# Where 15 late additions of a bias row stand in VectorE's order, in a linear attention kernel with a feed-forward layer behind it

## The chip, the cores and the metric

The kernel runs on one core of a Trainium2 chip. Its time is device microseconds (us) of one execution; lower is better. All times inside the execution are counted from the start of its span, the time from the first to the last instruction that the profiler recorded.

## The reference

Gated linear attention for 4 batches of 8 heads, 768 steps, head size 48, and then a feed-forward layer with a squared relu, on 3072 tokens of 384 values:

```python
for t in range(S):
    state = alpha[:, :, t, :, None] * state + np.einsum('bhd,bhe->bhde', k[:, :, t], v[:, :, t])
    y[:, :, t] = np.einsum('bhd,bhde->bhe', q[:, :, t], state)
x = y.transpose(0, 2, 1, 3).reshape(B * S, H * D)
h = x @ w_in                     # 384 -> 2048
r = np.maximum(h, 0.0)
g = s * (r * r) + b              # s and b are single numbers
out = g @ w_out                  # 2048 -> 384
```

The number b adds the same row to every token's output: b times the column sums of w_out. The kernel computes this **bias row** once and adds it to the 384 output values of each token.

## The kernel before

The 3072 tokens are 24 blocks of 128 tokens, six to a batch. Each block n passes through these steps; the names are those of the functions in the code, and each is a handful of instructions:

- **load** (SP's DMA queue): alpha, k, q and v of a block, into rings of eight buffers.
- **ln**, **cum_pe**, **cum_act**: ScalarE takes logarithms of alpha, TensorE sums them along the block (L283), ScalarE makes the decays b and 1/b from them (L296, L297). cum_act also sends the last row of the decays through DRAM (**decay**, and **decay_in** back into `blast`), for the state.
- **kb_mul**, **qb_mul** (VectorE, L345 and L348; "kb" and "qb" below): k times 1/b and q times b.
- **tr** (TensorE, L356) transposes qb and kb into the PSUM bank `ct_ps`; **qk_copy** (VectorE, L368) copies both out at once. The next cum_pe writes into the same bank, so it comes after that copy.
- **amat** (TensorE, L389): the products of k and q, from that copy; **mask** (VectorE, L398), twice.
- **y_pe**, **pst_pe** (TensorE, L503 and L516): the block's output and its contribution to the state; **y_act** (ScalarE); **t1** (VectorE, L575/577) and **sd** (GpSimd, L587 and L591) carry the state on. The last block of a batch (n = 5, 11, 17, 23) has no t1 and sd.
- **vcast** (GpSimd, L278): v in bf16.
- **xt_pe**, **xt_act**: the output is transposed for the feed-forward layer.
- **mp**, **rl**, **sq** for each quarter u = 0 to 3 of the 2048 inner values: TensorE multiplies by w_in (L601, 12 matmuls), ScalarE takes the relu (L614), VectorE squares (L621; "square (n, u)" below).
- **o_pe** (TensorE, L632, four matmuls for a quarter): multiplies the squares by w_out, into the bank `o_ps`.
- **o_out**: for n of 15 and more, VectorE adds the bias row to the result as it takes it out of PSUM (L649), and it is stored. The first 15 blocks are done before the bias row is known: ScalarE puts their results as they are into `keep_sb`, which lies where the first copy of w_in was (`w_in_st`). Later **add_bias** (VectorE, L683) adds the row to each of the 15, in place, and **store** sends it to DRAM. A store of blocks 0 to 3 takes two DMAs, since their rows lie interleaved.

The bias row comes about as follows, all on VectorE: **colsum** (L206) adds up the parts of w_out, 128 x 768 at a time, eight blocks of time apart; **bias_sum** (L209) adds the two halves; **bias_turn** (L213 to L221) sums over the partitions by way of transposes; **bias_out** and **bias_in** send the row through DRAM so that it stands on all partitions, in four parts; **bias_add** 0 and 1 (L236, L238) add these parts into `bias_w`.

The order of the work is written out by hand. `at(pos, function, ...)` notes an event at a position, in which a block is 8 wide; all events are sorted by position (at the same position: in the order in which they were noted) and carried out once, so that each engine's queue, SP's DMA queue among them, gets its instructions in this order. Every engine works through its own queue in order. From block 10 on, even and odd blocks have position tables of their own (`places`), which make a repeating pattern of two blocks. With the events of `at` and these tables, VectorE's queue from position 133 to 138 reads as follows before the change:

```
133.00 add_bias 0   133.29 qk_copy 18   134.34 sq 16 0   134.34 sq 16 2   134.36 o_out 15
134.95 kb_mul 19    134.95 qb_mul 19    135.54 sq 16 1   135.79 sq 16 3   136.66 add_bias 1   137.71 qk_copy 19
```

TensorE's queue in the same stretch is: o_pe (15, 2), mp (16, 0), mp (16, 2), o_pe (15, 3), cum_pe 19, mp (16, 1), mp (16, 3), y_pe 17, o_pe (16, 0), tr 19, o_pe (16, 1), xt_pe 17, amat 18, amat 19, o_pe (16, 2). The pairs 20/21 and 22/23 follow the same pattern, 16 positions later each, with pst_pe behind y_pe there, and t1 of the block before ahead of the odd block's qk_copy.

Of the kernel before, what the change touches and what calls it, by code (L numbers as in the profile page):

```python
# [14 lines left out]
def kernel(  # L15
# [109 lines left out]
    NKEEP = 15  # L125
    keep_all = w_in_st.rearrange("a t f -> a (t f)")
    keep_sb = [keep_all[:, d_model * n : d_model * (n + 1)] for n in range(NKEEP)]
# [627 lines left out]
    def at(pos, fn, *args):  # L755
        events.append((pos, len(events), fn, args))
# [54 lines left out]

    for i in range(3, 8):
        at(69.3 + 8 * (i - 3), colsum, i)
    at(103.3, bias_sum)
    at(110.0, bias_turn)
    at(110.3, bias_out)
    at(111.4, bias_in)
    at(128.5, bias_add, 0)
    at(130.5, bias_add, 1)
    for n in range(NKEEP):  # L820
        at(133.0 + 3.66 * n, add_bias, n)
        at(133.9 + 3.66 * n, store, n, keep_sb[n])

    def late(pos, *what):
        for fn, *args in what:
# [75 lines left out]
```

## Time and profile before

| what | value |
|---|---|
| median of 3 runs | 185.82 us (185.32 to 186.15) |
| the profiled execution | 185.98 us |
| its span | 184.2 us |
| granted TensorE clock, mean | 0.998 |
| DMA, share of the span that the 16 engines were busy (q1) | 71.6% |
| add_bias (L683) | 15 times, 541 to 741 ns, from 128.9 to 174.2 us |
| o_out of the late blocks (L649) | 8 times, 543 to 551 ns |
| colsum, 128 x 768 (L206) | 6 times, 943 to 952 ns |
| bias_add 0, bias_add 1 | 1.26 us at 126.83, 0.75 us at 128.12 |

In the rows of the timeline, the columns are start and duration in us, engine, line, operation, what is written from what is read, shapes, the count of instructions drawn together, and in brackets idle time of the engine before it with what ended it. Engines are PE (TensorE), DVE (VectorE), ACT (ScalarE), POOL (GpSimd) and SP. Durations of neighbours on one engine overlap, since an instruction begins while the one before it is still finishing; the spacing of the starts says what an instruction costs its engine.

### The profile page before, as it was taken

What the parts mean: (1) busy time and instruction counts of PE and PEld (TensorE: products, weight loads), DVE (VectorE), ACT (ScalarE), POOL (GpSimd) and SP (SyncE); (2) the same over time, 40 slices, a digit from 0 to 9 for tenths busy, and PEclk for the clock granted to TensorE, in tenths of its full rate; (3) what the DMA queues carried; (4) which work ended last, traced back from release to release, by engine and by line L of the source; (5) the groups of instructions that cost most, each with busy time, mean ns of one, the idle gap of its engine ahead of it and who ended that gap; (6) DMA issues with size and microseconds to landing.
All of it is one profiled execution on the core that took longest, in us unless ns stands there. A gap on an engine that the chain in (4) does not pass through costs nothing.

```text
span 184.2 us, 6231 instructions
## 1 busy us (share of the span) xinstructions
PE 177.9 (97%) x2504; PEld 142.2 (77%) x2504; DVE 145.8 (79%) x308; ACT 122.1 (66%) x253; POOL 61.4 (33%) x97
## 2 busy tenths in 40 slices
PE   7888999999999999999999999999999999999993
PEld 2556899866698687787888878888778878878793
DVE  7599879666657588987898997778999899896541
ACT  3779797985678956656766765765755746734750
POOL 7338481110330625042505344144203343344000
PEclk9999999999999999999999999999999999999999
DMA  5999989989488989892985671989685945233322
GB/s 151 314 327 350 232 282 382 279 176 186 75 162 154 202 161 189 161 174 52 164 147 113 110 127 57 244 151 176 150 172 131 174 134 175 73 101 112 94 63 76
DMA packets 105934, 31.12 MB, mean 169 GB/s; under 512 B 98595, under 2 KB 104370, under 8 KB 105906
## 3 DMA queue, kind: packets, MB, share of 16 engines
q1 hardware_dynamic: 105902, 30.73, 71.6%
q8 instruction: 19, 0.31, 0.7%
q14 instruction: 9, 0.07, 0.1%
q10 hardware_dynamic: 4, 0.00, 0.0%
HBM read 25.98 MB, written 4.75 MB: 167 GB/s over the span
## 4 chain that ended last, share of the span: by engine, by line
PE 82%; DVE 9%; ACT 4%; issue 2%; POOL 1%; ACTq 0%; DVEq 0%; POOLq 0%
PE h_ps L601 26%; PE o_ps L632 25%; PE ct_ps L356 4%; PE h_ps L632 3%; PE o_ps L257 2%; PE a_ps L601 2%; PE ct_ps L601 2%; PE y_ps L503 2%; PE a_ps L389 2%; DVE gt_all L621 2%; PE ct_ps L283 2%; PE h_ps L555 2%; ACT bi_sb L296 2%; PE o_ps L601 2%; DVE qb_sb L348 1%
## 5 line engine op out<-in xcount | busy, mean ns | idle before, releaser
L601 PEld LDWEIGHTS <-w_in_bf 128*128 128x128 bf16 x1152 | 67.5, 98 | 4.9 <-issue 0.7
L614 ACT ACTIVATE r_sb<-h_ps 128x512 bf16<-128x512 f32 x79 | 47.0, 604 | 31.2 <-PE h_ps L601 29.5
L632 PE MATMUL o_ps<-w_out_bf,gt_all 128*128 128x384 bf16 x320 | 64.0, 326 | 0.0
L601 PE MATMUL h_ps<-xd_all,w_in_bf 128*128 128x128 bf16 x948 | 60.3, 219 | 0.0
L587 POOL TENSOR_TENSOR sd_sb<-t_sb,blast 48x192 bf16<-48x192 f32 x40 | 28.7, 718 | 83.5 <-DVE t_sb L577 56.1
L621 DVE TENSOR_TENSOR gt_all<-r_sb 128x512 bf16<-128x512 bf16 x96 | 40.9, 443 | 15.4 <-ACT r_sb L614 14.9
L632 PEld LDWEIGHTS <-gt_all 128*128 128x128 bf16 x368 | 32.5, 98 | 15.3
L278 POOL CAST v_bf<-v_sb 128x384 bf16<-128x384 f32 x23 | 15.1, 667 | 23.3 <-DMA v_sb<-in_v_dram 23.1
L345 DVE TENSOR_TENSOR kb_sb<-k_sb,bi_sb 128x384 bf16<-128x384 f32 x24 | 14.2, 594 | 7.7 <-ACT bi_sb L296 7.7
L562 ACT ACTIVATE xd_all<-h_ps 128x384 bf16<-128x384 bf16 x19 | 9.6, 503 | 9.6 <-PE h_ps L555 9.6
L348 DVE TENSOR_TENSOR qb_sb<-q_sb,b_sb 128x384 bf16<-128x384 f32 x24 | 13.7, 573 | 1.6 <-ACT b_sb L297 1.6
L267 ACT ACTIVATE la_sb<-al_sb 128x384 bf16<-128x384 f32 x24 | 12.5, 532 | 2.3 <-DVE blast L748 2.3
L591 POOL TENSOR_TENSOR sc_sb<-t_sb,blast 112x384 f32<-112x384 f32 x16 | 13.3, 830 | 1.3
L525 ACT ACTIVATE y_bf<-y_ps 128x384 bf16<-128x384 f32 x22 | 10.9, 497 | 3.2 <-PE y_ps L503 2.8
L368 DVE COPY qkT<-ct_ps 112x1024 bf16<-112x1024 bf16 x16 | 10.9, 684 | 1.9 <-PE ct_ps L356 1.8
L398 DVE TENSOR_TENSOR am_a<-a_ps,mask 128x512 bf16<-128x512 f32 x13 | 8.9, 686 | 3.2 <-PE a_ps L389 3.0
L296 ACT ACTIVATE bi_sb<-ct_ps 128x384 f32<-128x384 f32 x19 | 9.3, 489 | 2.5 <-PE ct_ps L283 2.4
L356 PEld LDWEIGHTS <-qb_sb 128*112 128x112 bf16 x96 | 8.2, 130 | 3.3 <-DVE qb_sb L348 1.8
L398 DVE TENSOR_TENSOR am_b<-a_ps,mask 128x512 bf16<-128x512 f32 x13 | 8.9, 682 | 1.7 <-PE a_ps L389 1.7
L297 ACT ACTIVATE b_sb<-ct_ps 128x384 f32<-128x384 f32 x19 | 9.4, 497 | 0.0
L683 DVE TENSOR_TENSOR w_in_st<-w_in_st,bias_w 128x384 f32<-128x384 f32 x15 | 8.3, 560 | 0.0
L356 PEld LDWEIGHTS <-kb_sb 128*112 128x112 bf16 x96 | 7.2, 130 | 0.7 <-DVE kb_sb L345 0.4
(146 smaller groups left out, 256.9 us busy)
## 6 DMA issues: line engine op xcount, KB each, us to landing
al_sb<-in_alpha_dram SPq DMA_DIRECT2D x20, 192.0 KB, 4.1
q_sb<-in_q_dram SPq DMA_DIRECT2D x20, 192.0 KB, 4.4
k_sb<-in_k_dram SPq DMA_DIRECT2D x20, 192.0 KB, 3.5
v_sb<-in_v_dram SPq DMA_DIRECT2D x20, 192.0 KB, 3.9
w_in_st<-in_moe_w_in_dram SPq DMA_DIRECT2D x4, 768.0 KB
w_out_st<-in_moe_w_out_dram SPq DMA_DIRECT2D x4, 768.0 KB
out_dram<-w_in_st SPq DMA_DIRECT2D x11, 192.0 KB, 1.9
out_dram<-out_sb SPq DMA_DIRECT2D x10, 96.0 KB, 1.6
```

The lines of the kernel that those rows point to most:

```text
L278: nc.gpsimd.tensor_copy(out=v_bf[n % 4], in_=raw("v", n))
L296: nc.scalar.activation(out=bi_sb[n % 2], in_=cv, func=AF.Exp, scale=-1.0)
L345: nc.vector.tensor_tensor(out=kb_sb[n % 4][:, :, 0:48], in0=raw("k", n), in1=bi_sb[n % 2], op=ALU.mult)
L348: nc.vector.tensor_tensor(out=qb_sb[n % 2][:, :, 0:48], in0=raw("q", n), in1=b_sb[n % 3], op=ALU.mult)
L356: nc.tensor.transpose(out=t_bank(n, x if n in pair_of else None)[0:112, x, p, :], in_=t.rearrange("a h d -> a (h d)")[:, 128 * p : 128 * p ...
L398: nc.vector.tensor_tensor(out=am_sb[e][n % 2], in0=a_bank(n)[e], in1=mask4, op=ALU.mult)
L587: nc.gpsimd.tensor_tensor(out=sd[r, :, d], in0=t1_sb[r, :, d], in1=bl[r].to_broadcast([48, NP, 48]), op=ALU.mult)
L591: nc.gpsimd.tensor_tensor(out=sc_sb[0:112], in0=t1_sb[0:112], in1=bl[0:112].to_broadcast([112, NP, 96]), op=ALU.mult)
L601: nc.tensor.matmul(out=hp[:, jj * C : (jj + 1) * C], lhsT=w_in_bf[:, kk, 128 * j : 128 * (j + 1)], rhs=xd_sb[n][:, kk], start=(kk == 0), s ...
L614: nc.scalar.activation(out=rs, in_=room((g, u)), func=AF.Relu)
L621: nc.vector.tensor_tensor(out=gt_sb[g][:, u * 512 : (u + 1) * 512], in0=rs, in1=rs, op=ALU.mult)
L632: nc.tensor.matmul(out=op[:, 0:d_model], lhsT=gt_sb[n][:, j * C : (j + 1) * C], rhs=w_out_bf[:, j, :], start=(j == 0), stop=(j == NJ - 1),)
```

## The change

In position terms: bias_sum goes from 103.3 to 101.4, right behind the last colsum (101.3); bias_add 0 from 128.5 to 127.55, right ahead of kb_mul 18; bias_add 1 from 130.5 to 133.4, behind qk_copy 18. The 15 additions, which stood 3.66 positions apart from 133.0 on, get positions from a list, and each store stands 1.5 behind its addition instead of 0.9.

```diff
-    at(103.3, bias_sum)
+    at(101.4, bias_sum)
     at(110.0, bias_turn)
     at(110.3, bias_out)
     at(111.4, bias_in)
-    at(128.5, bias_add, 0)
-    at(130.5, bias_add, 1)
-    for n in range(NKEEP):
-        at(133.0 + 3.66 * n, add_bias, n)
-        at(133.9 + 3.66 * n, store, n, keep_sb[n])
+    at(127.55, bias_add, 0)
+    at(133.4, bias_add, 1)
+
+    spare = [134.9, 134.95, 135.0, 143.55, 150.9, 150.95, 151.0, 159.55, 166.9, 166.95, 167.0, 172.5, 175.5, 178.5, 181.5]
+    assert len(spare) == NKEEP
+    for n, pos in enumerate(spare):
+        at(pos, add_bias, n)
+        at(pos + 1.5, store, n, keep_sb[n])
```

By the sorting, VectorE's queue from 133.29 to 137.71 is then:

```
133.29 qk_copy 18   133.40 bias_add 1   134.34 sq 16 0    134.34 sq 16 2   134.36 o_out 15   134.90 add_bias 0
134.95 add_bias 1   134.95 kb_mul 19    134.95 qb_mul 19  135.00 add_bias 2   135.54 sq 16 1   135.79 sq 16 3
137.71 qk_copy 19
```

Additions 4 to 6 stand in the same way in the next pair and 8 to 10 in the one after it; 3 and 7 stand between o_out and kb_mul of the even blocks 20 and 22; 11 ahead of square (21, 0), 12 between o_out 20 and square (21, 2), 13 and 14 ahead of square (22, 0).

## The prediction

> **What bounds the kernel now.** I read the busy row first, then the waits and the order in time of TensorE, then the same of VectorE where TensorE was late.
>
> ```profile
> PE 177.9 (97%) x2504; PEld 142.2 (77%) x2504; DVE 145.8 (79%) x308; ACT 122.1 (66%) x253; POOL 61.4 (33%) x97
> ```
>
> TensorE is busy 97% of the span, so a moved VectorE instruction can only count through a hole that it opens or closes in TensorE's row. From 95 us on I compared every matmul's start with the one before (o_pe 0.162 us, mp 0.055 us each). Apart from steps of 0.06 to 0.10 where the kind of matmul changes, four places are late. Three of them, in TensorE's rows (start, duration, idle before):
>
> ```profile
> 130.30 0.32 PE L283 MATMUL ct_ps<-la_sb,U_bf 128*128 128x384 bf16 x1 [0.30 <-DVE qkT L368]
> ...
> 147.88 0.40 PE L389 MATMUL a_ps<-qkT 48*128 48x128 bf16 x8
> 148.22 0.23 PE L389 MATMUL y_ps<-qkT 48*128 48x128 bf16 x1
> ...
> 161.86 0.40 PE L389 MATMUL a_ps<-qkT 48*128 48x128 bf16 x8
> 162.37 0.23 PE L389 MATMUL y_ps<-qkT 48*128 48x128 bf16 x1
> ```
>
> At 130.30 cum_pe 19 waits for qk_copy 18; its four predecessors began at 129.19 and need 4 x 0.162, so it is 0.46 late. In pairs without a hole, amat of the odd block starts 0.23 after amat of the even one (134.19 and 134.42). At 148.22 it is 0.34 (0.11 late), at 162.37 it is 0.51 (0.28 late), at 106.39 it is 0.45 (0.22 late). All four are VectorE's copies of transposed q and k (L368). So 1.07 us is all that a better order of VectorE can win from 95 us on.
>
> Now VectorE before one of them (blocks 18 and 21):
>
> ```profile
> 143.39 1.17 DVE L621 TENSOR_TENSOR gt_all<-r_sb 128x512 bf16<-128x512 bf16 x2 [1.00 <-ACT r_sb L614]
> 144.48 0.54 DVE L649 TENSOR_TENSOR out_sb<-o_ps,bias_w 128x384 f32<-128x384 f32 x1
> 144.95 0.54 DVE L345 TENSOR_TENSOR kb_sb<-k_sb,bi_sb 128x384 bf16<-128x384 f32 x1
> 145.41 0.55 DVE L348 TENSOR_TENSOR qb_sb<-q_sb,b_sb 128x384 bf16<-128x384 f32 x1
> 145.88 0.54 DVE L683 TENSOR_TENSOR w_in_st<-w_in_st,bias_w 128x384 f32<-128x384 f32 x1
> 146.35 0.74 DVE L621 TENSOR_TENSOR gt_all<-r_sb 128x512 bf16<-128x512 bf16 x2
> 147.02 0.54 DVE L577 TENSOR_TENSOR t_sb<-p_ps,sc_sb 112x384 f32<-112x384 f32 x1
> 147.49 0.67 DVE L368 COPY qkT<-ct_ps 112x1024 bf16<-112x1024 bf16 x1
> ```
>
> There is idle time only before the squares of the even block (1.00, ended by the relu). From the second square to the end of the copy, 148.16, VectorE runs without a gap, and TensorE goes on at 148.22. I call this the **odd chain**: two squares, o_out, kb, qb, two squares, t1, qk_copy. It starts when relu (18, 2) ends, which the new order doesn't change, and it has no room: TensorE already waits 0.11 for it.
>
> **The change, part by part.** Spacing is from one start to the next: 0.47 for an add (145.88 to 146.35), o_out, kb, qb or t1; 0.33 for a square; 0.65 from qk_copy to what follows. An instruction on TensorE follows its input's end by 0.05 (162.32 to 162.37).
>
> *bias_sum* leaves the place ahead of square (12, 1), where it made qk_copy 15 late, for the 0.45 of idle after colsum 7 (101.00 to 101.45). It has 0.47 to give back, the hole is 0.22: at best -0.22. But GpSimd is at work there:
>
> ```profile
> 101.45 1.74 DVE L621 TENSOR_TENSOR gt_all<-r_sb 128x512 bf16<-128x512 bf16 x2 [0.45 <-ACT r_sb L614]
> ```
>
> Two squares take 1.74 instead of 0.74, while GpSimd's state multiply (L591) runs from 101.44 for 0.83. Each shift of these squares up to 0.26 is free, one of 0.47 uses up all that bias_sum gave back, and 0.1 more makes tr 15 late. Bounds -0.22 and +0.1; I take -0.1, the middle. The Trainium skill (SBUF — State Buffer, Who interferes with whom) says that a VectorE instruction with two SBUF inputs and a GpSimd one that reads SBUF exclude each other, whoever is first, for the whole instruction. The stretched squares agree; by this rule bias_sum pushes GpSimd's multiplies, and so the squares behind them, back by its own length, and the term would be 0 instead of the -0.22 that the idle row alone would give.
>
> *bias_add 0* goes ahead of kb 18, where VectorE is idle 0.82 before 124.72. It waits for the bias row, whose four loads were issued by 114.0 and took 3.5, so it is there by 117.6, 6 us early. It costs 0.95 (the same shape in the colsum at 100.05), so kb 18 moves by some 0.1 and tr 18, 1 us later, sees nothing. *bias_add 1* goes behind qk_copy 18, into the idle time before the squares. qk_copy 18 then starts when tr 18 is done, about 127.4 instead of 129.57, and the 0.46 hole at 130.30 closes.
>
> *add_bias 0 to 2, 4 to 6, 8 to 10* come in threes into the odd chains of the pairs 18/19, 20/21 and 22/23: two between o_out and kb, one behind qb. Each of these chains held one add before. So 0.94 more stands in each; the idle 1.00 lies ahead of the relu, and the adds lie behind it, so it hides nothing.
>
> - Pair 18/19 (the chain holds no t1). Relu (16, 2) ends at 130.05, so square (16, 2) starts at 130.08, o_out 130.42, adds 130.89 and 131.36, kb 131.83, qb 132.30, add 132.77, squares 133.24 and 133.57, qk_copy 133.90 to 134.58. TensorE, freed of its 0.46, would be at tr 19 at 132.37; qb ends at 132.84, so it starts at 132.89. o_pe (16, 1) was at 133.27 and now waits for square (16, 1), which ends at 133.65: 133.70, +0.43. Behind it xt and amat come without a wait. **+0.43**, the closed hole already counted.
> - Pair 20/21. Chain from square (18, 2) at 144.06 (relu ends at 144.03): o_out 144.40 (0.08 sooner than in the row, whose squares were stretched that much beside GpSimd), adds 144.87 and 145.34, kb 145.81, qb 146.28, add, squares 147.22 and 147.55, t1 147.88, qk_copy 148.35 to 149.03. amat 21 at 149.08 instead of 148.22: **+0.86**. Of it, tr 21 waits 0.44 first, o_pe (18, 1) 0.35 more.
> - Pair 22/23. Here the two squares took 0.70 and 0.67 instead of 0.42, beside GpSimd. Adds 8 and 9 ran beside GpSimd's state multiplies before it (1.08 and 1.05 for 0.50); they are moved away, so GpSimd is done sooner and I count 0.26 of relief, once, since the second square waits for its relu anyway: o_out at 158.38, qk_copy 162.33 to 163.01, amat 23 at 163.06 instead of 162.37: **+0.69**.
>
> *The rest* (adds 3, 7, 11 to 14) stands in even stretches or near the end: add 3 moves kb 20 by 0.21 where tr 20 is 1.0 later; 11 to 14 lie in idle times of 0.84 and 1.29. Nothing. What the old places give free also wins nothing beyond the four holes, as TensorE waits nowhere else.
>
> *Stores* go 1.5 behind their adds on SP. Stores 0 to 2 (six issues of 0.6 to 0.8) now stand ahead of decay 20 and load 23, where four stood: 1.4 later at most. Load 23's alpha then lands about 147 and is read at 153.4; the decay row lands about 150 and is read at 154.7. If that cover went, GpSimd's sd would be late, 4 us away. The last store stays.
>
> Sum: -0.1 + 0.43 + 0.86 + 0.69 = +1.88. The profiled execution took 185.98 (span 184.2 and 1.8 around it), so 187.86; the median of the runs is 0.16 lower, so I predict **187.7**.
>
> **The rivals.**
>
> 1. *The adds are hidden after all, not slower.* If the odd chain had 0.94 to spare, only the closed holes would count: 185.82 - 1.07 = 184.75. For it: 0.44 of idle before kb 17 at 117.08. Against: that pair has no o_out there, which takes 0.47, and TensorE follows qk_copy 21 and 23 by 0.05. It decides where an add in the chain costs under about 0.1. Chance 0.06.
> 2. *GpSimd's relief is larger.* The two squares of pair 22/23 were 0.28 and 0.25 longer; if 0.53 came back in every chain, pairs 18, 20 and 22 would cost -0.10, +0.41 and +0.42, and bias_sum -0.22: +0.5, 186.3. Against: in the other two pairs the squares are already short, or wait for the relu. Chance 0.09.
> 3. *The adds meet GpSimd.* add_bias 0 took 0.74 at 128.91, beside GpSimd, instead of 0.55. If one add in each three is spaced 0.74 instead of 0.47, +0.8: 188.5. Against: after its cast of v ends (144.28) GpSimd has nothing until t1. Chance 0.07.
>
> My forecast has the other 0.78, and of itself spans 187.1 (0.12 less at bias_sum; 0.1, 0.25 and 0.15 less in the pairs, should GpSimd's relief be felt there) to 188.2 (0.2 more at bias_sum, and the reliefs of 0.26 and 0.08 gone). The range reaches down to the second rival and up to the third: 186.3 to 188.5. Half a per cent, 0.93 us, is about what a measurement of this kernel can tell from no change: the first rival is faster (0.06), the second within it (0.09), forecast and third slower (0.85).
>
> **What would show it.** In the changed profile: no idle before cum_pe 19; bias_add 0 at 0.95; three L683 around each odd kb and qb; holes before tr 19, 21 and 23 (up to 0.5), before o_pe of the even block's second quarter (0.35), before amat 21 and 23, each ended by VectorE; together 2 to 2.8 us. If amat 21 starts within 0.3 of amat 20 and tr 21 doesn't wait, my chain is wrong. I am also wrong if relu (18, 2) is no longer what starts it.

## The result, and the profile after

The changed kernel took 187.68 us in the median of 7 runs (186.97 to 187.96), the kernel before 185.89 (185.32 to 187.03): a ratio of 1.0084, with a 95% interval of 1.0055 to 1.0113. It is slower by 0.84%. The profiled execution has a span of 185.9 us instead of 184.2. Medians here are of all executions, while ratios leave out the few slow ones, in which the granted TensorE clock was lower (0.97 in the mean; in the profiled execution of experiment 3 it was 0.86 and 0.88 in the first two stretches of 20 us, and 1.00 from there on).

First TensorE around the cum_pe 19 that used to be late, and the odd block 19 behind it (start, duration, what, idle before it and who ended that):

```profile
128.91 0.81 PE L632 MATMUL o_ps<-w_out_bf,gt_all 128*128 128x384 bf16 x4
129.56 0.33 PE L283 MATMUL ct_ps<-la_sb,U_bf 128*128 128x384 bf16 x1
...
132.62 0.43 PE L356 MATMUL ct_ps<-ident,qb_sb 128*112 128x128 bf16 x4 [0.37 <-DVE qb_sb L348]
...
133.43 0.82 PE L632 MATMUL o_ps<-w_out_bf,gt_all 128*128 128x384 bf16 x4 [0.15 <-DVE gt_all L621]
```

cum_pe 19 now starts 0.65 behind the first of the four o_pe matmuls, without a hole. In its place there are two new ones: tr 19 waits for qb, o_pe for the square of the second quarter. The bracket shows less than what is lost, since the ends of matmuls are modelled; by the spacing of the starts tr is 0.53 late and o_pe 0.32. Pair 20/21 has the same two (0.36 and 0.32), and a third hole, of 0.24, before amat 21; pair 22/23 repeats these three sizes. So eight holes with 2.69 us stand where four with 1.07 stood:

```profile
147.04 0.43 PE L356 MATMUL ct_ps<-ident,qb_sb 128*112 128x128 bf16 x4 [0.20 <-DVE qb_sb L348]
...
147.85 0.82 PE L632 MATMUL o_ps<-w_out_bf,gt_all 128*128 128x384 bf16 x4 [0.15 <-DVE gt_all L621]
148.77 0.40 PE L389 MATMUL a_ps<-qkT 48*128 48x128 bf16 x8
149.25 0.23 PE L389 MATMUL y_ps<-qkT 48*128 48x128 bf16 x1
```

And VectorE's odd chain before it:

```profile
143.55 0.43 DVE L621 TENSOR_TENSOR gt_all<-r_sb 128x512 bf16<-128x512 bf16 x1 [1.32 <-ACT r_sb L614]
144.22 0.42 DVE L621 TENSOR_TENSOR gt_all<-r_sb 128x512 bf16<-128x512 bf16 x1 [0.24 <-ACT r_sb L614]
144.56 0.55 DVE L649 TENSOR_TENSOR out_sb<-o_ps,bias_w 128x384 f32<-128x384 f32 x1
145.03 1.02 DVE L683 TENSOR_TENSOR w_in_st<-w_in_st,bias_w 128x384 f32<-128x384 f32 x2
145.97 0.55 DVE L345 TENSOR_TENSOR kb_sb<-k_sb,bi_sb 128x384 bf16<-128x384 f32 x1
146.43 0.55 DVE L348 TENSOR_TENSOR qb_sb<-q_sb,b_sb 128x384 bf16<-128x384 f32 x1
146.90 0.56 DVE L683 TENSOR_TENSOR w_in_st<-w_in_st,bias_w 128x384 f32<-128x384 f32 x1
```

The idle time before the first square has even grown, from 1.00 to 1.32, while the three additions stand behind the squares, where there was no idle time.

The first 106 us of a profiled execution vary by more than the terms here (amat 14 began between 105.28 and 106.84 in the kernels below, in one of them at 110.09). So beside each time I give **the stretch** from the start of amat 14 to the end of TensorE's last matmul, in which all that was changed lies, but for bias_sum's own instruction. It is 75.37 us before (105.94 to 181.31) and 77.14 after (105.89 to 183.04): +1.77.

### The profile page after: what moved, and what is told of

The parts are those of the page before. It is cut to its first block, busy times and chain, and to the rows that moved or that the text cites. A ratio compares the mean times of both kernels' runs of the same rounds, so it can differ in the third digit from the quotient of the medians.

```text
span 185.9 us, 6230 instructions
## 1 busy us (share of the span) xinstructions
PE 178.7 (96%) x2504; PEld 142.0 (76%) x2504; DVE 144.6 (78%) x308; ACT 122.1 (66%) x253; POOL 60.2 (32%) x97
## 4 chain that ended last, share of the span: by engine, by line
PE 82%; DVE 10%; ACT 4%; issue 2%; POOL 1%; DVEq 0%; ACTq 0%; POOLq 0%
PE h_ps L601 25%; PE o_ps L632 25%; PE ct_ps L356 4%; PE h_ps L632 3%; DVE w_in_st L683 2%; PE o_ps L257 2%; ACT r_sb L614 2%; PE a_ps L601 2%; PE ct_ps L601 2%; PE a_ps L389 2%; PE y_ps L503 2%; PE h_ps L555 2%; PE o_ps L601 1%; PE a_ps L658 1%; PE a_ps L632 1%
## 5 line engine op out<-in xcount | busy, mean ns | idle before, releaser
L587 POOL TENSOR_TENSOR sd_sb<-t_sb,blast 48x192 bf16<-48x192 f32 x40 | 25.1, 626 | 90.8 <-DVE t_sb L577 51.9
L278 POOL CAST v_bf<-v_sb 128x384 bf16<-128x384 f32 x23 | 16.8, 742 | 18.9 <-DMA v_sb<-in_v_dram 18.8
L591 POOL TENSOR_TENSOR sc_sb<-t_sb,blast 112x384 f32<-112x384 f32 x16 | 14.0, 877 | 1.3
L356 PE MATMUL ct_ps<-ident,qb_sb 128*112 128x128 bf16 x72 | 7.2, 222 | 0.8 <-DVE qb_sb L348 0.8
```

What stands on the lines that cost most here:

```text
L278: nc.gpsimd.tensor_copy(out=v_bf[n % 4], in_=raw("v", n))
L356: nc.tensor.transpose(out=t_bank(n, x if n in pair_of else None)[0:112, x, p, :], in_=t.rearrange("a h d -> a (h d)")[:, 128 * p : 128 * p ...
L587: nc.gpsimd.tensor_tensor(out=sd[r, :, d], in0=t1_sb[r, :, d], in1=bl[r].to_broadcast([48, NP, 48]), op=ALU.mult)
L591: nc.gpsimd.tensor_tensor(out=sc_sb[0:112], in0=t1_sb[0:112], in1=bl[0:112].to_broadcast([112, NP, 96]), op=ALU.mult)
```

## The experiments

In the experiments, each ratio is against the kernel before, run again beside it (median 186.15 us for 1, 3, 4 and 5, 186.14 for 6 and 7).

The theory: an addition costs when it stands in an odd chain, between the relu that starts it and qk_copy, and nothing in VectorE's idle time. The rivals: SP's order of stores, GpSimd, or only the additions that tr waits for.

**1. The nine additions ahead of the even block's squares**; the stores keep their positions by a list of their own.

```diff
-    spare = [134.9, 134.95, 135.0, 143.55, 150.9, 150.95, 151.0, 159.55, 166.9, 166.95, 167.0, 172.5, 175.5, 178.5, 181.5]
+    spare = [134.3, 134.31, 134.32, 143.55, 150.3, 150.31, 150.32, 159.55, 166.3, 166.31, 166.32, 172.5, 175.5, 178.5, 181.5]
```

> The changed kernel with its nine additions 0 to 2, 4 to 6, 8 to 10 ahead of the even block's squares, where VectorE waits 0.85, 1.32 and 1.32 us for the relu; stores and everything else stay. Chain theory (the additions cost because they stand between the relu that starts the odd chain and qk_copy): all holes before tr, o_pe and amat of the odd blocks go, in pair 18/19 the second square comes 0.16 later without effect; what is left are the gains, 1.07 against the kernel before: 184.8 us. Rival, the stores' new order on SP's queue costs: unchanged from the changed kernel, 187.7. Rival, GpSimd: the additions now run beside its state multiplies, are stretched to 0.74 or push the squares by 0.3 in each pair: 185.2 to 185.7.

Measured: 185.74 us, ratio 0.9977 (0.9955 to 0.9998); stretch 75.01, 0.36 less than before. The loss is gone with the stores where the changed kernel has them, so SP is out as its cause. But two thirds of the 1.07 didn't come: tr 19 still waits 0.29, and amat 21 and 23 start 0.10 late. VectorE and then GpSimd, ahead of kb 21:

```profile
141.82 1.48 DVE L683 TENSOR_TENSOR w_in_st<-w_in_st,bias_w 128x384 f32<-128x384 f32 x3
143.23 1.69 DVE L621 TENSOR_TENSOR gt_all<-r_sb 128x512 bf16<-128x512 bf16 x2
```

```profile
140.65 3.02 POOL L587 TENSOR_TENSOR sd_sb<-t_sb,blast 48x192 bf16<-48x192 f32 x2 [11.04 <-DVE t_sb L575]
143.75 0.89 POOL L591 TENSOR_TENSOR sc_sb<-t_sb,blast 112x384 f32<-112x384 f32 x1
```

GpSimd needed this idle time: its two multiplies take 3.02 instead of 1.08 in the best case (119.42 before), the next begins only at 143.75, and the squares behind the additions then take 1.69 for 0.76. This agrees with the Trainium skill (SBUF — State Buffer, Who interferes with whom): VectorE with two SBUF inputs and a reading GpSimd shut each other out. That whoever is first goes first, as the prediction has it from there, these rows don't show: the second multiply began at 141.33, before the first addition (141.82), yet each addition took its usual 0.55 and the multiply 2.34. The rival that names GpSimd had nearly the right size (185.2 to 185.7, measured 185.74).

**2. Experiment 1 without GpSimd's sc for the blocks 18 and 20.**

```diff
-        if c < NCH - 2:
+        if c < NCH - 2 and n not in (18, 20):
```

> The kernel with the nine additions ahead of the even block's squares, and without GpSimd's state multiply into sc (L591) for the blocks 18 and 20: that part of the state is left out. If GpSimd's held-up work is what stretched the squares of block 18 (0.73 and 1.02 us there), they take 0.43 again, amat 21 starts 0.23 to 0.26 behind amat 20 instead of 0.34, and the wait of 0.29 before tr 19 stays, since there it is GpSimd's cast of v that meets the additions: about 0.2 less than that kernel, 185.5 us. Rival, the squares wait for the additions alone: durations of 0.7 and 1.0 stay.

Measured, in a single execution: 184.57 us, stretch 74.65, 0.36 less than experiment 1, where about 0.2 was expected. amat 21 follows amat 20 without a hole, and tr 19 waits 0.29, as expected. The squares are better, but not at 0.43:

```profile
142.41 1.37 DVE L621 TENSOR_TENSOR gt_all<-r_sb 128x512 bf16<-128x512 bf16 x2
```

By the rows the first still meets the late multiply into sd, the second the cast of v (0.73 and 0.71). So GpSimd's held-up work stretches the squares: for sc that is shown, for sd and the cast it is read from these rows.

**3. Two additions in each odd chain instead of three**; their stores go with them.

```diff
-    spare = [134.9, 134.95, 135.0, 143.55, 150.9, 150.95, 151.0, 159.55, 166.9, 166.95, 167.0, 172.5, 175.5, 178.5, 181.5]
+    spare = [134.9, 134.95, 138.0, 143.55, 150.9, 150.95, 154.0, 159.55, 166.9, 166.95, 170.0, 172.5, 175.5, 178.5, 181.5]
```

> The changed kernel with one of the three additions of each odd chain (2, 6 and 10, those behind qb) moved behind qk_copy, ahead of the masks. Chain theory: the holes before tr 19, 21 and 23 stay (0.53, 0.36, 0.36), those before o_pe (0.32 each) go, amat 21 and 23 wait 0.1 instead of 0.24: 0.32, 0.47 and 0.47 less, so 186.4 us. Rival, only the two additions ahead of kb count: 187.7.

Measured: 186.72 us, ratio 1.0041 (1.0012 to 1.0070). Its profiled execution was held up by 4 us before amat 14, so only the stretch is read: 75.87, +0.50 against the kernel before; the +0.51 behind the expected 186.4 was the same. The holes before tr stay (0.53, 0.36, 0.36), those before o_pe are gone.

**4. All three additions behind qb, none ahead of kb**; the stores as in experiment 1.

```diff
-    spare = [134.9, 134.95, 135.0, 143.55, 150.9, 150.95, 151.0, 159.55, 166.9, 166.95, 167.0, 172.5, 175.5, 178.5, 181.5]
+    spare = [134.96, 134.97, 135.0, 143.55, 150.96, 150.97, 151.0, 159.55, 166.96, 166.97, 167.0, 172.5, 175.5, 178.5, 181.5]
```

> The changed kernel with all three additions of each odd chain behind qb, none ahead of kb. Chain theory: tr 19, 21 and 23 no longer wait, but the squares end when they did, so o_pe of the second quarter takes over the whole wait, and amat 21 and 23 start when they did: 187.7 us, no change from the changed kernel. Rival, only the two additions ahead of kb count, since tr waits first: the holes go, 185 to 186.

Measured: 188.36 us, ratio 1.0115 (1.0085 to 1.0146), and the stretch is 77.14, that of the changed kernel. tr 21 doesn't wait any more, and o_pe takes over its wait:

```profile
147.25 0.39 PE L356 MATMUL ct_ps<-ident,qb_sb 128*112 128x128 bf16 x4
147.47 0.39 PE L356 MATMUL ct_ps<-ident,kb_sb 128*112 128x128 bf16 x4
148.41 0.82 PE L632 MATMUL o_ps<-w_out_bf,gt_all 128*128 128x384 bf16 x4 [0.56 <-DVE gt_all L621]
```

So where in the chain an addition stands moves the hole and leaves its size. The median is 0.7 above that of the changed kernel and the 187.7 expected. In the profiled executions the spans differ by 0.56, which lies before amat 14 (106.46 instead of 105.89); the kernel before also took 0.26 more beside this run (186.15 instead of 185.89), and the intervals of the two ratios overlap.

**5. The bias row's steps alone**, additions and stores as before.

Against the kernel before:

```diff
-    at(103.3, bias_sum)
+    at(101.4, bias_sum)
...
-    at(128.5, bias_add, 0)
-    at(130.5, bias_add, 1)
+    at(127.55, bias_add, 0)
+    at(132.9, bias_add, 1)
```

> The kernel before with the bias row's steps alone moved: bias_sum and bias_add 0 as in the change, bias_add 1 ahead of the first addition (132.9), additions and stores as before. Chain theory: the holes at 106.39 (0.22) and 130.30 (0.46) go, those of 0.11 and 0.28 before amat 21 and 23 stay: 0.68 less than before, 185.2 us. Rival, these steps win nothing since TensorE meets the next wait at once: 185.9.

Measured: 185.18 us, ratio 0.9947 (0.9921 to 0.9973); stretch 74.69, 0.68 less than before. The holes of 0.11 and 0.28 are there, the other two are gone.

**6. Without the nine additions.**

```diff
-        at(pos, add_bias, n)
+        if n not in (0, 1, 2, 4, 5, 6, 8, 9, 10):
+            at(pos, add_bias, n)
```

> The changed kernel without the nine additions of the odd chains (blocks 0 to 2, 4 to 6 and 8 to 10 are stored without the bias row); their stores stay. Chain theory: no hole before tr, o_pe or amat of the odd blocks, squares of 0.43: the gains alone, 184.8 us, 2.85 less than the changed kernel, so the nine additions cost 0.32 each. Rival, stores or loads on SP cost a part: 185.5 to 187.7 with the holes gone.

Measured: 184.75 us, ratio 0.9919 (0.9902 to 0.9935); stretch 74.27, 1.10 less than before and 2.87 less than the changed kernel: 0.32 for each of the nine additions, in the mean. No hole that VectorE ends is left.

**7. The additions spread over VectorE's idle times.**

```diff
-    spare = [134.9, 134.95, 135.0, 143.55, 150.9, 150.95, 151.0, 159.55, 166.9, 166.95, 167.0, 172.5, 175.5, 178.5, 181.5]
+    spare = [138.0, 143.55, 150.3, 154.0, 159.55, 170.0, 172.5, 175.5, 178.5, 181.5, 183.5, 187.5, 187.6, 187.7, 187.8]
...
-        at(pos + 1.5, store, n, keep_sb[n])
+        at(pos + 0.5, store, n, keep_sb[n])
```

> The changed kernel with the 15 additions at other places: none in an odd chain; one ahead of the masks of each pair (0.45 of idle), one ahead of kb of the blocks 20 and 22, one ahead of the squares of block 18, and ten in the idle times from square (21, 0) on, the last four ahead of square (23, 0), where VectorE waits 2.36 us; each store 0.5 behind its addition. Chain theory: no hole that VectorE ends is left, the gains alone remain, 1.07 less than the kernel before: 184.8 us, 0.4 better than moving the bias row's steps alone. Rival, the late stores collide with the last output: 185.5 or more, with a longer way from the last addition to the end than 2.5 us.

Measured: 185.06 us, ratio 0.9949 (0.9931 to 0.9967). The stretch is 74.27, exactly that of experiment 6, so the nine additions that 6 leaves out cost nothing here; and none of the 15 opens a hole (nine of them, not ten, stand from square (21, 0) on). amat 20 and 21 of this kernel:

```profile
147.20 0.40 PE L389 MATMUL a_ps<-qkT 48*128 48x128 bf16 x8
147.44 0.22 PE L389 MATMUL y_ps<-qkT 48*128 48x128 bf16 x1
```

One addition does meet GpSimd, the one ahead of the squares of block 18:

```profile
141.31 0.55 DVE L683 TENSOR_TENSOR w_in_st<-w_in_st,bias_w 128x384 f32<-128x384 f32 x1
142.71 1.34 DVE L621 TENSOR_TENSOR gt_all<-r_sb 128x512 bf16<-128x512 bf16 x2 [0.85 <-ACT r_sb L614]
```

```profile
140.14 2.09 POOL L587 TENSOR_TENSOR sd_sb<-t_sb,blast 48x192 bf16<-48x192 f32 x2 [10.98 <-DVE t_sb L575]
```

The multiplies take 2.09 and the squares 1.34, and yet amat 21 isn't late. One addition fits at this place, three (experiment 1) don't. The last four additions, and the end:

```profile
173.15 1.96 DVE L683 TENSOR_TENSOR w_in_st<-w_in_st,bias_w 128x384 f32<-128x384 f32 x4
175.59 0.43 DVE L621 TENSOR_TENSOR gt_all<-r_sb 128x512 bf16<-128x512 bf16 x1 [0.49 <-ACT r_sb L614]
...
180.27 0.36 DVE L667 TENSOR_TENSOR out_sb<-a_ps,bias_w 128x192 f32<-128x192 f32 x1 [0.30 <-PE a_ps L658]
```

There is idle time left behind them, and from the end of VectorE's last instruction (180.63; it adds the bias row to the last output, L667) to the span's end (183.1) it is 2.5, as before (181.71 to 184.2). By its ratio this kernel is 0.5% faster than the kernel before, and so faster than the changed one. By medians it can't be told from experiment 5; in the stretch it is 0.42 shorter, about the two holes that 5 keeps (0.11 and 0.28).

From one even amat to the next, by the number of additions in the odd chain:

| additions in the chain | amat 18 to 20 | amat 20 to 22 |
|---|---|---|
| 0 (experiment 7) | 13.69 | 13.87 |
| 1 (before) | 13.69 | 13.98 |
| 2 (experiment 3) | 14.10 | 14.37 |
| 3 (changed kernel) | 14.42 | 14.85 |

The first nearly fits (0 and 0.11); each further one costs 0.32 to 0.48, 0.40 in the mean, of its 0.47 on VectorE. The wait before amat 21 falls into the second column, which therefore grows more.

## Why the prediction was right, point by point

The sum holds: -0.21 + 0.44 + 0.86 + 0.70 is +1.79 by the parts below, the stretch has +1.77, the medians differ by 1.79, and the forecast was +1.88. That the median then came out at 187.68 against 187.7 is partly luck: the kernel before came out 0.07 above the 185.82 that the forecast started from, and the change 0.09 below its +1.88. The eight holes that the prediction named are there, with 2.69 us of the 2 to 2.8 that it gave.

- **What bounds the kernel**: right. The 1.07 in four holes was nearly all that an order of VectorE won here: with no addition in a chain the stretch is 1.10 shorter.
- **bias_sum**: I took -0.1 between -0.22 and +0.1; measured -0.21, as amat 15 follows amat 14 by 0.24. GpSimd did stretch it (0.75 instead of 0.55), and the squares behind it were 0.20 later by the start of kb 15, within the 0.26 that I had called free. GpSimd's multiply into sd, at work since 99.52, ended when it had ended before (101.32 and 101.37), and it was bias_sum that took longer beside it; so the squares did not move by bias_sum's own length, and the term was not the 0 that the prediction set beside it either. This term was the one mis-sized (and the middle of its bounds is -0.06, not the -0.1 taken).
- **bias_add 0 and 1**: right. bias_add 0 took 0.95 at 123.54 and kb 18 followed at 124.45; the 0.46 hole closed, and experiment 5 gives -0.68 for these steps together.
- **Pair 18/19**: +0.43 forecast. amat 19 started at 134.59 instead of 134.42, and tr 18 ahead of it 0.27 sooner: +0.44.
- **Pair 20/21**: +0.86 forecast. amat 21 at 149.25 instead of 148.22, less the 0.17 it came with: +0.86. Its first part was smaller than written: tr 21 waited 0.36, not 0.44; the prediction's own rows (qb ends at 146.83, tr 21 was at 146.51) give 0.37.
- **Pair 22/23**: +0.69 forecast. amat 23 at 164.10 instead of 162.37, less 1.03: +0.70. The relief was there: its two squares took 0.42 and 0.43.
- **The rest and the stores**: right that they cost nothing; experiment 6 keeps additions 3, 7 and 11 to 14 and all stores, and has no hole.
- **The rivals**: no idle time hid the nine additions where they stand (first rival), and no addition was stretched there (third; all 15 took 0.55). GpSimd's relief was no larger than counted (second): the pairs cost 0.44, 0.86 and 0.70, not the -0.10, 0.41 and 0.42 of that rival. The third's mechanism is real, but for another order: in experiment 1, whose stretch is 0.74 longer than that without the nine additions, experiment 2 gives 0.36 of it to sc; for the 0.29 before tr 19, where two additions took 0.75 and 0.85 beside the casts of v, it is only argued from these rows.

The medians of experiments 6 and 7 differ by 0.3 with equal stretches; their executions cover nearly the same range (184.26 to 185.77 and 184.34 to 185.76), so this is no difference that the runs can tell.

## What to carry to other kernels

Idle time of an engine is worth something only at the place where it lies: ask what ends it, and put work ahead of that event, not behind it. Where one engine is busy 97% of the time, list the few places where its starts are late and follow back the chain to each; in such a chain, once its room is used up, a further instruction costs most of its length (here 0.32 to 0.48 for 0.47), wherever in it it stands. Then ask who uses the idle time already: ahead of the even block's squares it was GpSimd.

## What the runs showed that I had not expected

In experiment 1 GpSimd got no turn between three additions that stood back to back: its second multiply into sd, begun at 141.33, ended at 143.67 and took 2.34 instead of 0.50, through the three additions and into the square behind them.

This is no rule, though. Some 13 us earlier in the same run GpSimd's casts of v did get in between additions. VectorE and then GpSimd:

```profile
128.50 1.99 DVE L683 TENSOR_TENSOR w_in_st<-w_in_st,bias_w 128x384 f32<-128x384 f32 x3
```

```profile
127.83 1.78 POOL L278 CAST v_bf<-v_sb 128x384 bf16<-128x384 f32 x2
```

Here the three additions take 1.99 instead of the 1.48 above. The second cast began at 128.78 and ended at 129.61, while the second addition, begun at 129.17, took 0.85. What decides who goes first is not shown, and the profile's times on GpSimd are rough.
